# Where the P products of an attention-plus-FFN kernel run: two runs of 1024 columns a batch in place of four of 512

## The chip, the cores and the metric

The kernel runs on one core of one Trainium2 chip. The metric is the device time of one execution in microseconds (us). Before the change it is 701.11 us, the median of three runs that lie between 700.99 and 701.15 us.

## The reference

Eight batches of compressed-memory attention with 8 heads feed a feed-forward layer with SiLU:

```python
a = softmax(phi, over the sequence)             # phi: (8, 8, 576, 32)
k_m = einsum('bhsm,bhsd->bhmd', a, k)           # (8, 8, 32, 64)
v_m = einsum('bhsm,bhsd->bhmd', a, v)
attn = softmax(q @ k_m.T / sqrt(64))            # (8, 8, 576, 32)
x = attn @ v_m                                  # to (4608, 512)
h = x @ w_in                                    # (512, 2048)
out = (h * sigmoid(h)) @ w_out                  # (2048, 512)
```

All data are float32. The weights reach the chip as 64-bit words, which the kernel turns into float32 during the first batch.

## The kernel before, in words

**The algebra.** The kernel never forms x. For a batch b it forms P = v_m @ w_in, head by head: a matrix of 256 rows (8 heads of 32 memories) and 2048 columns, the hidden width. Then h = attn @ P. Each float32 factor of the two big products is split into a rounded part and a remainder ("hi" and "lo", type fp32r), and hi·hi + hi·lo + lo·hi is added up in PSUM.

**One iteration.** The work of a batch is 16 iterations, fc = 0 to 15, each for 128 hidden columns. On TensorE (PE) an iteration is, in program order:

1. `ffn1(b, fc)` (L637): 12 matmuls of 288 columns into the tile `h`, which is two PSUM banks; only columns 0 to 287 of each bank are used. There is one buffer of `h`, so the next `ffn1` waits until all readers of this one are done.
2. The events of the slots (b, fc) and (b, fc + 0.5): small steps that prepare this and the next batch.
3. `finish` (L676, `ffn2`): 12 matmuls of 512 columns for the iteration before, into four PSUM banks `acc`.

In batch 0 the order differs a little: half of `finish` comes before the events of part 0 and half before those of part 1. After each odd batch four more groups ("left", `accleft`) handle the 64 rows of two batches that the 512-row main part leaves over.

ScalarE (ACT) runs `silu`: L660 on the first 256 columns of both banks, then L662 on the last 32 (`gleft`). VectorE (DVE) makes hi (L652) and lo (L654) of the result, `gparts`. PE's instructions keep the program's order; from batch 1 on ACT's do too. DVE's order is drawn up by a scheduler at compile time, which may move an instruction ahead of one that was traced before it.

**The P products.** `p_mm(b, f, w)` (L602) makes w columns of P: 8 matmuls with 64-row, 32-column tiles of the array (4 head pairs by 2), run by PE as 16 instructions, into the two banks of the tile `bg`. `p_split` then has ACT copy them to hi (L616) and DVE subtract to get lo (L618), into `pparts`, which holds two blocks of 512 columns. A block j (512 columns) is used by `ffn1` of fc = 4j to 4j + 3.

**The slots.** From batch 1 on, block j = 1, 2, 3 is made at slot 4j − 3, that is at 1, 5 and 9, and block 0 of the next batch n = b + 1 at slot 14. For the next batch there are also, from batch 1 on, in slot 5 `e_mm` (L322, L330: k_m and v_m), in slot 9 `e_tr` (L352: their transposes), in slot 10 `s_all` (L367: the scores), in slot 12 `s_max` and `s_sub`, then `s_exp` (13), `s_sum`, `s_norm`, and in slot 14 `s_back` (L442, L443) and `s_low` (L448). In slots 5 and 9 the P product is registered first, so on PE it stands ahead of `e_mm` and of `e_tr`.

**Beside h.** `e_mm`, `e_tr` and part of `s_all` write into the unused columns of the same `h` tile that `ffn1` of that iteration has just filled:

```python
    def beside_h(w):
        return [live["h"][:, i, HALF : HALF + w] for i in range(2)]
```

Tiles are guarded by whole PSUM banks. In the built program the first matmul of `e_mm`, of `e_tr` and of the part of `s_all` beside h carries a wait for the L662 of the same iteration (ACT's last read of those banks).

**Stores.** `store` (L683) has ACT copy an `acc` bank to a tile `o`, one of three buffers that the raw weights used in batch 0, and the SP queue sends it out.

**The start.** In the first 30 us, products with an identity tile (`keep_warm`, L79) stand on PE wherever it waits for the first batch's attention; the longest such wait holds 13 of them (line 815).

Of the kernel before, what the change touches and what calls it, by code (L numbers as in the profile page):

```python
# [10 lines left out]
F32 = mybir.dt.float32  # L11
F32R = mybir.dt.float32r
# [7 lines left out]
P = 128  # L20
# [4 lines left out]
DMODEL, DFF = 512, 2048  # L25
NFC = DFF // P
CW = 256
JW = 512
NJ = DFF // JW
# [3 lines left out]
NI = MAIN // P  # L33
# [8 lines left out]
RAWB = 3  # L42
# [6 lines left out]
def attn_ffn_kernel(  # L49
# [9 lines left out]
    nc = tc.nc  # L59
    const = ctx.enter_context(tc.tile_pool(name="const", bufs=1))  # L60
    sb = ctx.enter_context(tc.tile_pool(name="sb", bufs=2))
    ps = ctx.enter_context(tc.tile_pool(name="ps", bufs=1, space=bass.MemoryType.PSUM))
# [4 lines left out]
    dummy = ident.bitcast(mybir.dt.bfloat16)  # L67
# [4 lines left out]
    gparts = const.tile([P, 2, 2, MAIN], F32R, name="gparts")  # L72
    gleft = const.tile([P, NFC, 2 * LEFT], F32, name="gleft")
    aparts = const.tile([P, 2, 2, 2 * S], F32R, name="aparts")
    pparts = const.tile([P, 2, 2, 2 * JW], F32R, name="pparts")

    def keep_warm(t, n):
        for _ in range(n):
            nc.tensor.matmul(  # L79
                t, dummy[:, :P], dummy.unsqueeze(1).broadcast_to([P, 2, 2 * P]),  # L80
                start=True, stop=True, skip_group_check=True,
            )

    loads = []

# [28 lines left out]
    def bgtile():  # L114
        return ps.tile([P, 2, 512], F32, tag="bg", name="bg", bufs=1)
# [96 lines left out]
    def load_phi(b):  # L212
        t = sb.tile([P, PHW], F32, tag="att", name=f"phi{b}")
        at[b]["e"] = t[:, : FULLC * HM].rearrange("p (g c f) -> p g c f", g=2, c=FULLC)
        at[b]["er"] = t[:, FULLC * HM :]
        at[b]["et"] = t
        w = FULLC * P
        for f in ((0, w), (2 * w, PHW), (w, 2 * w)) if b == 0 else ((0, PHW),):
            load(t[:, f[0] : f[1]], phi[b, :, f[0] : f[1]], queue=nc.scalar if f[0] == w else None)
# [367 lines left out]

    pj = {}  # L590

    def p_mm(b, f, w, low=True):
        j = f // JW
        if f % JW == 0:
            pj[b, j] = [pparts[:, k, j % 2].rearrange("p (g f) -> p g f", g=2) for k in range(2)]
        hi, lo = pj[b, j]
        c = slice(f % JW, f % JW + w)
        bg = bgtile()
        kvT = at[b]["kvT"]
        for r in range(NR):  # L600
            for p in range(2):
                nc.tensor.matmul(  # L602
                    bg[M * r : M * (r + 1), p, :w].rearrange("p (k f) -> p k f", f=P),
                    kvT[D * p : D * (p + 1), 1, r],
                    win[D * p : D * (p + 1), f // P : (f + w) // P, r],
                    start=True, stop=True, skip_group_check=True,
                )
        if low:
            p_split(b, f, w, bg)
        return bg  # L610

    def p_split(b, f, w, bg, steps=(0, 1)):
        hi, lo = pj[b, f // JW]
        c = slice(f % JW, f % JW + w)
        if 0 in steps:
            nc.scalar.activation(hi[:, :, c], bg[:, :, :w], AF.Copy)  # L616
        if 1 in steps:
            nc.vector.tensor_tensor(lo[:, :, c], bg[:, :, :w], hi[:, :, c], op=ALU.subtract)  # L618
# [47 lines left out]
            last_silu.append(i)  # L666
        return g32

    acc = {}

    def ffn2(gs, cs, fc, key):
        ghi, glo = gs
# [5 lines left out]
            )  # L678

    def store(key, rows, last=False):  # L680
        o = sb.tile([P, DMODEL], F32, tag="raw", name="o", bufs=RAWB)
        a = acc.pop(key)
        nc.scalar.activation(o, a, AF.Copy)  # L683
        at_ = 0
        for k, (r, n) in enumerate(rows):
            (nc.scalar if last and k else nc.sync).dma_start(out[r : r + n], o[at_ : at_ + n])
            at_ += n
# [17 lines left out]
    def ev(b, slot, fn, *a):  # L705
        events.setdefault((b, slot), []).append((fn, a))

    for b in range(B):
        n = b + 1
        if b == 0:  # L710
            for j in range(2, DFF // CW):
                ev(b, 2 * j - 1.5, p_mm, b, j * CW, CW)
        else:
            for j in range(1, NJ):
                ev(b, 4 * j - 3, p_mm, b, j * JW, JW)
        if n == B:
            continue
        at_slot = (4, 5, 6, 7.5, 9, 9.5, 11.5, 12.5, 13, 13.5, 13.5, 14) if b == 0 else (1, 2, 3, 5, 9, 10, 10, 11, 12, 13, 13, 14)
        mx, sub, ex, em, tr, s0, s1, sx, se, ss, sn, sk = at_slot
        ev(b, mx, phi_max, n)  # L720
        if n == 1:
            ev(b, sub, phi_allmax, n, (0, 1), (0,))
            ev(b, sub + 0.5, phi_allmax, n, (0, 1), (1,))
        else:
            for i in range(3):
                ev(b, sub, phi_fold, n, i)
        ev(b, sub + 0.5, phi_sub, n)
        ev(b, ex, phi_exp, n)
        ev(b, em, e_mm, n)
        if n + 1 < B:  # L730
            ev(b, 14 if b == 0 else em + 1, load_kv, n + 1)
        ev(b, tr, e_tr, n)
        ev(b, em, load_q, n, 1)
        if n == 1:
            ev(b, s0, s_mm, n, 0)
            ev(b, s1, s_mm, n, 1)
        else:
            ev(b, s0, s_all, n)
        if n + 1 < B:
            ev(b, s1, load_q, n + 1, 0)  # L740
        ev(b, sx, s_max, n, ALL)
        ev(b, sx, s_sub, n, ALL)
        ev(b, se, s_exp, n, ALL)
        ev(b, ss, s_sum, n, ALL)
        ev(b, sn, s_norm, n, ALL)
        ev(b, sk, s_back, n, ALL)
        ev(b, sk, s_low, n, ALL)
        if n + 1 < B:
            ev(b, sk, load_phi, n + 1)
        ev(b, 14, p_mm, n, 0, JW)  # L750
    slots = [1.5, 1.5] + [2 * j - 1 if k == "i" else min(2 * j - 0.5, 12.5) for k, i in later for j in [i - 1 if k == "i" else i]]
    to_do = list(slots)
    for slot in slots:
# [14 lines left out]
    with in_order(DVE, ACT) as last:  # L768
        load_phi(0)
        nc.scalar.activation(tiny[:, :1], ident[:, :1], AF.Exp)  # L770
        load_kv(0)
        for c in LOADS.split():
            if c[0] == "Q":
                load_q(0, int(c[1]), True)
            elif c[0] == "L":
                load_next(True)
            else:
                w_load((c[0], 0), int(c[1]), True)
        keep_warm(idle, 10)
        phi_max(0, (0,))  # L780
        phi_allmax(0, (0,))
        phi_max(0, (1,))
        keep_warm(idle, 3)
        phi_sub(0, (0,))
        phi_allmax(0, (1,))
        phi_sub(0, (1,))
        for p in range(2):
            phi_exp(0, (p,))
        keep_warm(idle, 2)
        e_mm(0)  # L790
        w_conv(I0, 0, "pc")
        keep_warm(idle, 3)
        f_tr()
        f_vt()
        w_conv(I0, 0, "s")
        keep_warm(idle, 2)
        f_scores(0)
        f_copy(0)
        w_conv(I0, 0, "a")
        spare = ps.tile([P, 512], F32, tag="acc", name="spare", bufs=NI)  # L800
        keep_warm(spare, 2)
        f_turn(0)
        f_scores(1)
        f_max(0)
        f_copy(1)
        f_sub(0)
        keep_warm(spare, 3)
        f_turn(1)
        f_exp(0)
        w_conv(I0, 1, "pc")  # L810
        f_max(1)
        f_sub(1)
        f_exp(1)
        nc.scalar.activation(tiny[:, :1], ident[:, :1], AF.Silu)
        keep_warm(spare, 13)
        f_sum(0)
        f_norm(0)
        w_conv(I0, 1, "sa")
        f_back(0)
        f_sum(1)  # L820
        w_conv(O0, 0, "p")
        f_high(0)
        w_conv(O0, 0, "c")
        keep_warm(spare, 3)
        bg = p_mm(0, 0, CW, False)
        keep_warm(spare, 5)
        p_split(0, 0, CW, bg, (0,))
        w_conv(I1, None, "p")
        f_norm(1)
        f_back(1)  # L830
        f_low(0)
        p_split(0, 0, CW, bg, (1,))
        f_high(2)
        f_high(1)
        w_conv(O0, 0, "sh")
        f_low(1)
        f_low(2)
        w_conv(O0, 0, "a")
        h = ffn1(0, 0, low_last=True)
        g32 = silu(0, 0, h)  # L840
        w_conv(I1, None, "cs")
        gs = split(g32, steps=(0,))
        w_conv(O0, 0, "l")
        split(g32, steps=(1,), gs=gs)
        g32 = silu(0, 1, ffn1(0, 1, bgtile()))
        w_conv(I1, None, "a")
        w_conv(O0, 1, "pc")
        main_step(0, 0, gs, (0, 1))
        g1 = split(g32, steps=(0,))
        w_conv(O0, 1, "s")  # L850
        p_mm(0, CW, CW)
        w_conv(O0, 1, "h")
        main_step(0, 0, gs, (2, 3))
        split(g32, steps=(1,), gs=g1)
        w_conv(O0, 1, "al")
        prev = ("main", 0, 1, g1)
# [25 lines left out]
    for b in range(B):  # L882
# [3 lines left out]
        for fc in range(NFC):  # L886
# [5 lines left out]
            h = ffn1(b, fc)  # L892
            gs = split(silu(b, fc, h))
            for part in range(2):
# [3 lines left out]
                n = len(traced)  # L898
# [72 lines left out]
```

## Time and profile before

| what | value |
|---|---|
| median of three runs | 701.11 us |
| span of the profiled execution | 700.3 us (the rest of its time, some 0.8 us by the median, lies around the span) |
| mean granted TensorE clock | 0.998 |
| PE busy | 689.4 us (98%) |
| DVE busy | 365.4 us (52%) |
| ACT busy | 259.0 us (37%) |
| DMA, mean | 86 GB/s |
| L676 main / L637 / left L676, share of the chain that ended last | 45% / 25% / 6% |
| L602 (P) busy | 35.8 us |

A row of the timeline gives the start and duration in us, engine, line, operation, out<-in with shapes, and the count of merged instructions; brackets name idle time of that engine just before, and what ended it. Matmuls are pipelined and their ends are modelled, so the time that a group takes from PE is read from its start to the next group's start, not from its duration. PEld is the weight load, which overlaps PE.

### The profile page before, as it was taken

How to read it: one execution, taken by the hardware profiler on the slowest of the kernel's cores; microseconds unless marked ns; L12 is line 12 of the kernel's file. 1: busy time of each engine (PE TensorE's matmuls, PEld its weight loads, DVE VectorE, ACT ScalarE, POOL GpSimd, SP SyncE). 2: the span in 40 equal slices, each digit the busy share in tenths (PEclk: the TensorE clock that was granted, in tenths of full speed). 3: DMA queues.
4: the chain of work that ended last, by engine and by line, in shares of the span. 5: the costliest groups of instructions: out<-in, count | busy, mean ns of one | idle time of the engine just before them, and what ended most of it. 6: DMA issues, size and time to landing. Idle time of an engine off the chain costs nothing.

```text
span 700.3 us, 11773 instructions
## 1 busy us (share of the span) xinstructions
PE 689.4 (98%) x4924; PEld 562.4 (80%) x4924; DVE 365.4 (52%) x665; ACT 259.0 (37%) x456; POOL 0.7 (0%) x6
## 2 busy tenths in 40 slices
PE   7999999999999999999999999999999999999997
PEld 3578777888888888888888888888888888888886
DVE  4898797435654256534636346542564525623322
ACT  3879584422424224421423314342241413431211
POOL 0000000000000000000000000000000000000000
PEclk9999999999999999999999999999999999999999
DMA  9995752212201221132110311112121000010002
GB/s 334 317 338 187 254 212 95 78 61 68 92 19 46 92 68 44 52 137 69 35 61 16 137 56 47 61 54 83 68 80 31 1 1 1 1 61 1 1 0 76
DMA packets 25445, 60.15 MB, mean 86 GB/s; under 512 B 2096, under 2 KB 10416, under 8 KB 25392
## 3 DMA queue, kind: packets, MB, share of 16 engines
q1 hardware_dynamic: 24448, 56.63, 22.8%
q10 hardware_dynamic: 944, 2.77, 1.1%
q8 instruction: 39, 0.64, 0.4%
q14 instruction: 14, 0.11, 0.1%
HBM read 49.95 MB, written 9.44 MB: 85 GB/s over the span
## 4 chain that ended last, share of the span: by engine, by line
PE 84%; DVE 2%; issue 0%; ACT 0%; ACTq 0%
PE acc L676 45%; PE h L637 25%; PE accleft L676 6%; PE bg L602 4%; PE h L322 2%; PE bg L367 1%; DVE wo_lo L176 0%; DVE raw L172 0%; PE h L330 0%; PE h L352 0%; DVE aparts L448 0%; DVE aT L442 0%; DVE gparts L654 0%; DVE sc L415 0%; DVE smx L411 0%
## 5 line engine op out<-in xcount | busy, mean ns | idle before, releaser
L676 PE MATMUL acc<-wo_hi,gparts 128*128 128x512 f32 x1024 | 341.8, 395 | 0.1
L676 PEld LDWEIGHTS acc<-wo_hi,gparts 128*128 128x128 f32 x1024 | 192.0, 188 | 52.7 <-issue 6.6
L637 PEld LDWEIGHTS h<-aparts,pparts 128*128 128x128 f32 x1524 | 214.0, 188 | 14.4 <-issue 2.1
L637 PE MATMUL h<-aparts,pparts 128*128 128x288 f32 x1524 | 223.3, 295 | 0.7 <-ACT aparts L581 0.4
L660 ACT ACTIVATE g<-h 128x512 f32<-128x512 f32 x127 | 76.0, 599 | 345.9 <-PE h L637 180.3
L676 PE MATMUL acc<-wo_lo,gparts 128*128 128x512 f32 x512 | 200.8, 392 | 0.7 <-DVE wo_lo L176 0.6
L652 DVE CAST gparts<-g 128x512 fp32r<-128x512 f32 x128 | 54.4, 425 | 260.0 <-ACT g L660 260.0
L676 PEld LDWEIGHTS acc<-wo_lo,gparts 128*128 128x128 f32 x512 | 96.1, 188 | 18.4 <-DVE wo_lo L176 1.9
L654 DVE TENSOR_TENSOR gparts<-g,gparts 128x512 fp32r<-128x512 f32 x128 | 88.2, 689 | 10.3
L618 DVE TENSOR_TENSOR pparts<-bg,pparts 128x1024 fp32r<-128x1024 f32 (+1 forms) x36 | 39.7, 1102 | 5.4 <-ACT pparts L616 5.0
L676 PE MATMUL accleft<-wo_hi,gparts 128*128 128x512 f32 x128 | 40.6, 389 | 0.0
L616 ACT ACTIVATE pparts<-bg 128x1024 fp32r<-128x1024 f32 (+1 forms) x36 | 33.6, 932 | 14.8 <-PE bg L602 14.8
L602 PE MATMUL bg<-win,kvT 64*32 64x512 f32 (+1 forms) x576 | 35.8, 554 | 0.0
L676 PEld LDWEIGHTS accleft<-wo_hi,gparts 128*128 128x128 f32 x128 | 24.0, 188 | 4.9
L662 ACT ACTIVATE gleft<-h 128x64 f32<-128x64 f32 x127 | 27.8, 219 | 0.0
L683 ACT ACTIVATE o<-acc 128x512 f32<-128x512 f32 x32 | 19.2, 600 | 21.8 <-PE acc L676 10.6
L676 PE MATMUL accleft<-wo_lo,gparts 128*128 128x512 f32 x64 | 24.9, 389 | 0.0
L660 ACT ACT_TABLE_LOAD x14 | 18.0, 1283 | 14.2 <-issue 13.6
L652 DVE CAST gparts<-gleft 128x512 fp32r<-128x512 f32 x16 | 6.8, 427 | 20.7 <-PE accleft L676 12.2
L168 ACT ACTIVATE raw<-raw 128x1024 int32<-128x1024 uint32 (+1 forms) x16 | 16.8, 1048 | 0.0
L322 PEld LDWEIGHTS h<-kv,phi 128*32 128x32 f32 x384 | 10.2, 110 | 5.0 <-ACT gleft L662 5.0
L676 PEld LDWEIGHTS accleft<-wo_lo,gparts 128*128 128x128 f32 x64 | 12.0, 188 | 2.4
(139 smaller groups left out, 365.0 us busy)
## 6 DMA issues: line engine op xcount, KB each, us to landing
kv<-in_kv SPq DMA_DIRECT2D x28, 516.0 KB, 5.9
q<-in_q SPq DMA_DIRECT2D x16, 576.0 KB, 5.7
out<-o SPq DMA_DIRECT2D x32, 256.0 KB, 2.1
raw<-in_w_in SPq DMA_DIRECT2D x14, 512.0 KB, 6.6
raw<-in_w_out SPq DMA_DIRECT2D x6, 1024.0 KB, 5.5
phi<-in_phi SPq DMA_DIRECT2D x7, 576.0 KB, 3.8
kv<-in_kv ACTq DMA_DIRECT2D x4, 516.0 KB, 6.8
kr<-in_kv SPq DMA_DIRECT2D x7, 258.0 KB, 6.4
```

Source lines behind the costliest of these rows:

```text
L168: nc.scalar.activation(r, low, AF.Copy, scale=2.0**-29)
L322: nc.tensor.matmul(pt[p][M * r : M * (r + 1), :KVW], e[:, p, c, M * r : M * (r + 1)], kvt[c][:, p, r], start=c == 0, stop=False, skip_grou ...
L602: nc.tensor.matmul(bg[M * r : M * (r + 1), p, :w].rearrange("p (k f) -> p k f", f=P), kvT[D * p : D * (p + 1), 1, r], win[D * p : D * (p + ...
L616: nc.scalar.activation(hi[:, :, c], bg[:, :, :w], AF.Copy)
L618: nc.vector.tensor_tensor(lo[:, :, c], bg[:, :, :w], hi[:, :, c], op=ALU.subtract)
L637: nc.tensor.matmul(h[:, hf, :HALF], wt[:, p, fs], a[:, p, hf * HALF : (hf + 1) * HALF], start=n[hf] == 0, stop=n[hf] == 5, skip_group_chec ...
L652: nc.vector.tensor_copy(ghi, g32)
L654: last_split.append(nc.vector.tensor_tensor(glo, g32, ghi, op=ALU.subtract))
L660: nc.scalar.activation(g32.rearrange("p (h f) -> p h f", h=2), h[:, :, :w], AF.Silu)
L662: i = nc.scalar.activation(gleft[:, fc, o : o + LEFT].rearrange("p (h f) -> p h f", h=2), h[:, :, w:HALF], AF.Silu)
L676: nc.tensor.matmul(acc[key], gt[:, cs], wt[:, fc], start=fc == 0 and n == 0, stop=fc == NFC - 1 and n == 2)
L683: nc.scalar.activation(o, a, AF.Copy)
```

## The change

1. From batch 1 on P is made in runs of two blocks. `p_run(b, j)` sends the 16 instructions of block j into `bg` and the 16 of block j + 1 into a newly allocated `h` tile, all 512 columns of each bank; then block j + 1 is split first (so that `h` comes free) and block j second. `p_run(b, 2)` stands in slot 6 of batch b; `p_run(n, 0)` for the next batch in slot 12 (slot 14 of batch 0). Nothing is made any more in slots 1, 5, 9 and (after batch 0) 14. Batch 0's own P products are unchanged.
2. Blocks 0 and 1 have a home of their own (`early`, two of the three raw-weight buffers); blocks 2 and 3 stay in `pparts`.
3. `store` uses four fixed quarters of the third raw-weight buffer in turn.
4. The 13 identity products of line 815 are replaced by 16 products of zeros or of 96 identity columns, of 128 to 512 columns each, and two identity products; GpSimd (POOL) zeroes a part of `gparts` for them at the start.

```diff
+    nc.gpsimd.memset(gparts[:, 0, 0].bitcast(F32), 0.0)
+    zeros = gparts[:, 0, 0]
...
+    def zero_mm(t, k, n, w):
+        a = dummy if k == "half" else zeros
+        m = 96 if k == "half" else P
+        b = dummy.unsqueeze(1).broadcast_to([P, 2, 2 * P]) if k == "half" else zeros[:, :w]
+        for _ in range(n):
+            nc.tensor.matmul(t[:m, :w], a[:, :m], b, start=True, stop=True, skip_group_check=True)
...
-    pj = {}
-
-    def p_mm(b, f, w, low=True):
+    pj, early = {}, []
+
+    def p_home(b, j):
+        if b and j < 2:
+            if not early:
+                early.extend(sb.tile([P, 2, 2 * JW], F32R, tag="raw", name=f"pe{k}", bufs=RAWB) for k in range(2))
+            home = [early[k][:, j] for k in range(2)]
+        else:
+            home = [pparts[:, k, j % 2] for k in range(2)]
+        pj[b, j] = [x.rearrange("p (g f) -> p g f", g=2) for x in home]
+
+    def p_run(b, j):
+        bg = p_mm(b, j * JW, JW, False)
+        h = p_mm(b, (j + 1) * JW, JW, False, ps.tile([P, 2, 512], F32, tag="h", name="hp", bufs=1))
+        p_split(b, (j + 1) * JW, JW, h)
+        p_split(b, j * JW, JW, bg)
+
+    def p_mm(b, f, w, low=True, bg=None):
...
     def store(key, rows, last=False):
-        o = sb.tile([P, DMODEL], F32, tag="raw", name="o", bufs=RAWB)
+        if not homes:
+            homes.append(sb.tile([P, NI, DMODEL], F32, tag="raw", name="o", bufs=RAWB))
+        o = homes[0][:, next(stored) % NI]
...
         else:
-            for j in range(1, NJ):
-                ev(b, 4 * j - 3, p_mm, b, j * JW, JW)
+            ev(b, 6, p_run, b, 2)
...
+        PR = 14 if b == 0 else 12
...
+        ev(b, PR, p_run, n, 0)
         ev(b, sx, s_max, n, ALL)
         ev(b, sx, s_sub, n, ALL)
...
-        ev(b, 14, p_mm, n, 0, JW)
...
-        keep_warm(spare, 13)
+        zero_mm(spare, "full", 3, 512)
+        zero_mm(spare, "full", 4, 256)
+        zero_mm(spare, "half", 3, 512)
+        zero_mm(spare, "full", 3, 288)
+        zero_mm(spare, "full", 3, 128)
+        keep_warm(spare, 2)
```

More of the change, by code (lines that the diff above doesn't have):

```diff
@@ L586, in attn_ffn_kernel @@
     ALL = (0, S)
-    pj = {}
-    def p_mm(b, f, w, low=True):
+    pj, early = {}, []
[13 more added lines that the diff above has]
+    def p_mm(b, f, w, low=True, bg=None):
         j = f // JW
         if f % JW == 0:
[L595 to L598, printed above, removed]
+            p_home(b, j)
+        if bg is None:
+            bg = bgtile()
         kvT = at[b]["kvT"]
@@ L667, in silu @@
         return g32
-    acc = {}
+    acc, homes, stored = {}, [], iter(range(1 << 30))
     def ffn2(gs, cs, fc, key):
```

## The prediction

> **What bounds the kernel now.** I read the page first, then the table of windows, then PE's timeline around the places that the change touches, and last the waits of PE's weight loads.
>
> ```profile
> PE 689.4 (98%) x4924; PEld 562.4 (80%) x4924; DVE 365.4 (52%) x665; ACT 259.0 (37%) x456; POOL 0.7 (0%) x6
> ```
>
> ```profile
> 180.00:260.00 80.00, 80.00 (x568) 66.91 (x568) 37.16 (x73) 22.18 (x44) 0.00 (x0) 1.00 0.20 69
> 260.00:340.00 80.00, 80.00 (x590) 66.74 (x589) 40.28 (x77) 28.91 (x51) 0.00 (x0) 1.00 0.19 66
> ```
>
> PE is busy for all 80.00 us of a window of 80, at a granted clock of 1.00, while DVE and ACT stand idle half the time and more. So whatever PE does, or waits for, is paid in full, and whatever shortens only DVE, ACT or a queue gives nothing. The question is then how many microseconds each placed P product takes from PE, and this is read from start to start. First a plain iteration, then one with a P product alone (slot 1), in PE's timeline:
>
> ```profile
> 275.74 1.75 PE L637 MATMUL h<-aparts,pparts 128*128 128x288 f32 x12
> 277.33 0.39 PE L676 MATMUL acc<-wo_hi,gparts 128*128 128x512 f32 x1
> ...
> 280.07 1.74 PE L637 MATMUL h<-aparts,pparts 128*128 128x288 f32 x12
> 281.74 1.09 PE L602 MATMUL bg<-win,kvT 64*32 64x512 f32 x16
> 282.76 0.50 PE L676 MATMUL acc<-wo_hi,gparts 128*128 128x512 f32 x1
> ...
> 285.61 1.75 PE L637 MATMUL h<-aparts,pparts 128*128 128x288 f32 x12
> ```
>
> The plain iteration takes 280.07 − 275.74 = 4.33 us. With P it is 5.54, so P costs 1.21: entry 0.08 (1.67 to P instead of 1.59), body 1.02, exit 0.11 (2.85 to the next L637 instead of 2.74). Next, the same for slot 5 (P, then `e_mm`) and slot 9 (P, then `e_tr`):
>
> ```profile
> 131.79 1.74 PE L637 MATMUL h<-aparts,pparts 128*128 128x288 f32 x12
> 133.46 1.09 PE L602 MATMUL bg<-win,kvT 64*32 64x512 f32 x16
> 134.48 1.97 PE L322 MATMUL h<-kv,phi 128*32 128x129 f32 x64
> ...
> 139.63 0.42 PE L637 MATMUL h<-aparts,pparts 128*128 128x288 f32 x2
> ```
>
> ```profile
> 152.61 1.74 PE L637 MATMUL h<-aparts,pparts 128*128 128x288 f32 x12
> 154.28 1.09 PE L602 MATMUL bg<-win,kvT 64*32 64x512 f32 x16
> 155.30 0.44 PE L352 MATMUL h<-ident,kvn 128*128 128x128 f32 x2
> ...
> 158.33 0.42 PE L637 MATMUL h<-aparts,pparts 128*128 128x288 f32 x2
> ```
>
> These iterations take 7.84 and 5.72 us, 3.51 and 1.39 over the plain one. The four P slots of a batch (1, 5, 9, 14) cost 1.21 + 3.51 + 1.39 + 1.21 = 7.32, `e_mm` and `e_tr` included.
>
> **The cover that the move takes away.** Three narrow windows on PE, ACT's timeline of the same iteration, and the waits of the weight loads:
>
> ```profile
> 154.06 0.29 PE L637 MATMUL h<-aparts,pparts 128*128 128x288 f32 x1
> 154.28 0.66 PE L602 MATMUL bg<-win,kvT 64*32 64x512 f32 x8
> 154.73 0.64 PE L602 MATMUL bg<-win,kvT 64*32 64x512 f32 x8
> ```
>
> ```profile
> 154.93 0.22 ACT L662 ACTIVATE gleft<-h 128x64 f32<-128x64 f32 x1
> 155.47 1.03 ACT L616 ACTIVATE pparts<-bg 128x1024 fp32r<-128x1024 f32 x1 [0.33 <-PE bg L602]
> ```
>
> ```profile
> PEld h L322 <- ACT gleft L662: 5.0, 6, 0.8
> PEld h L352 <- ACT gleft L662: 5.0, 6, 0.8
> ```
>
> `e_mm` and `e_tr` write into banks that L660 and L662 still read, and wait for L662: in all six batches their weight load follows 0.8 us of idle time that L662 ended. L662 ends at 155.15, that is 1.09 after the start of the last L637 matmul (154.06). The P product runs from 154.28 to 155.30 and covers all of this. So P in slots 5 and 9 takes time that PE could not have used for the step behind it. In the changed kernel no P stands there, and since PE keeps program order nothing else can slip in. How soon PE follows L662 is seen at batch 1's start, where PE did idle for it:
>
> ```profile
> 107.90 0.22 ACT L662 ACTIVATE gleft<-h 128x64 f32<-128x64 f32 x1
> ```
>
> ```profile
> 108.17 0.53 PE L637 MATMUL h<-aparts,pparts 128*128 128x288 f32 x2
> 108.97 1.60 PE L637 MATMUL h<-aparts,pparts 128*128 128x288 f32 x10 [0.26 <-DVE aparts L448]
> ```
>
> 108.12 to 108.17: 0.05. So `e_mm` alone starts 1.09 + 0.05 = 1.14 after the last L637 start; behind P it started 1.24 after it (0.22 + 1.02). Removing P saves 0.10 in slot 5, not 1.02, and the same in slot 9: 3.41 and 1.29 remain. The lower bound of these two is an unhindered start, 2.49 and 0.29 (P's 1.02 gone, in slot 9 the entry too); the upper one 0.1 more in each, if changing the tile shape takes its 0.08 to 0.12 again after the wait. I take the wait without that, since the built program has it and the array can be drained by then.
>
> The Trainium skill, "PSUM — Partial Sum Buffer", section "PSUM bank collisions raise a hardware error", says that the chip does not arbitrate two engines on one bank and quadrant, disjoint columns included, so a semaphore must keep them apart. By that rule this wait cannot be scheduled away, and the trace agrees (155.15 before 155.30).
>
> **What a run of two costs.** One pass of 8 instructions takes 154.73 − 154.28 = 0.45 us, and behind the last pass 0.57, so 0.12 drains. A run is 0.08 + 4 × 0.45 + 0.12 + 0.11 = 2.12, against 2 × 1.21 apart: 0.30 saved. Its second half needs `h` free, at 1.14 by the same count, and the first half ends at 0.22 + 0.91 = 1.13. I add 0.05 (0.01 if weights load ahead, 0.11 if an entry is paid again): 2.17.
>
> Behind it the next `ffn1` needs `h` back. The copy starts 0.17 after the stream ends (155.47 against 155.30), takes 1.03, and DVE's subtraction takes 1.22:
>
> ```profile
> 135.71 1.22 DVE L618 TENSOR_TENSOR pparts<-bg,pparts 128x1024 fp32r<-128x1024 f32 x1 [0.24 <-ACT pparts L616]
> ```
>
> With two hand-overs of 0.05 that is 2.52 after the stream's end, and PE has 2.85 of L676 to do: 0.33 to spare, so nothing is added from batch 1 on.
>
> **Batch 0.** The run in slot 14 adds two passes, 0.91. But there only six L676 stand between it and the next `ffn1`, from 102.14 to 103.64:
>
> ```profile
> 101.13 1.09 PE L602 MATMUL bg<-win,kvT 64*32 64x512 f32 x16
> 102.14 0.50 PE L676 MATMUL acc<-wo_hi,gparts 128*128 128x512 f32 x1
> ...
> 103.64 1.75 PE L637 MATMUL h<-aparts,pparts 128*128 128x288 f32 x12
> ```
>
> ```profile
> 104.29 0.68 DVE L654 TENSOR_TENSOR gparts<-g,gparts 128x512 fp32r<-128x512 f32 x1
> 104.89 1.43 DVE L442 STREAM_TRANSPOSE aT<-sc 128x576 f32<-128x576 f32 x2
> 106.25 1.18 DVE L618 TENSOR_TENSOR pparts<-bg,pparts 128x1024 fp32r<-128x1024 f32 x1
> 107.56 1.36 DVE L448 TENSOR_TENSOR aparts<-aT,aparts 128x1152 fp32r<-128x1152 f32 x1
> ```
>
> PE would reach `ffn1` at 104.55. The run ends at 101.13 + 1.92 = 103.05, the copy at 104.25. DVE's subtraction stands behind L654 (the code ties it there in batch 0), so it runs from 104.97 to 106.19 and PE goes on at 106.24: 1.7 us lost. If the scheduler leaves L442 ahead of it, as before, 3.0; if it goes ahead of L654, 1.0. The chain through L442 and L448 to batch 1's first `ffn1` moves by about as much as PE does, so I add nothing there.
>
> **The small edits.** Stores: four buffers should end ACT's waits for outgoing DMAs, but PE hardly noticed them:
>
> ```profile
> PEld acc L676 <- ACT o L683: 0.8, 1, 0.8
> ```
>
> With no P in slot 1 PE needs `acc` 1.2 us sooner, and without the DMA wait it is free sooner too. Nothing. The raw buffers that `early` takes are last read by batch 0's weight conversion, which stands ahead of L654 on DVE; I add nothing for them. The zero products stand in a wait that a DVE chain ends:
>
> ```profile
> 18.62 2.97 PE L79 MATMUL spare<-ident 128*128 128x512 bf16 x13
> 22.46 0.63 PE L563 MATMUL firsta<-ident,fsc 128*128 128x128 f32 x4 [0.87 <-DVE fsc L556]
> ```
>
> PE is idle for 0.87 us behind them. 18 products at 0.23 each, the rate of a full L676, would be 4.1 of the 3.84 there: at most +0.3, and many are narrower, so zero. POOL's one fill (its whole busy time is 0.7) is ready long before 18 us.
>
> **The sum**, against the profiled execution's span of 700.3:
>
> - Batches 1 to 6, each: 2 × 2.17 + 3.41 + 1.29 = 9.04 for 7.32, +1.72; six times: +10.3.
> - Batch 7 (slots 1, 5, 9 had P alone): 2.17 for 3.63: −1.5.
> - Batch 0: +0.9 and +1.7.
>
> Together +11.4: a span of 711.7. The median of 701.11 stands 0.8 above the span, so 712.5.
>
> **Rivals.**
>
> 1. *The waits do not bite* (faster). If `e_mm` and `e_tr` could start at once, and `h` came back in time in batch 0 too, a batch costs 2 × 2.12 + 2.49 + 0.29 = 7.02, −0.30; six of these, −1.5 of batch 7 and +0.9 of batch 0 give −2.4: 698.7. With batch 0's stall 700.4. It decides if PE starts L322 and L352 less than 0.3 us behind L637. For it speaks only that no iteration of before shows PE itself idle there; against it the twelve waits above. A rule for it is in the Trainium skill, "TensorEngine Tiling (Array Packing)", section "Key Properties": changing the tiling mode drains TensorE. By it fewer changes of mode are a gain, and the trace agrees on their price (0.08 to 0.12 each); it does not see the cover.
> 2. *`h` comes back late in every run* (slower still). The spare is 0.33. If DVE is in the middle of a long step when the copy ends, up to 1.36 − 0.33 = 1.0 is lost; with this in the six slot-12 runs, 718.5. `s_max` and `s_sub` are traced right behind that run, but before they ran far earlier, in slots 10 and 11:
>
> ```profile
> 163.54 1.35 DVE L411 TENSOR_REDUCE smx<-sc 128x36 f32<-128x1152 f32 x1
> 164.92 1.36 DVE L415 TENSOR_TENSOR sc<-sc,smx 128x1152 f32<-128x1152 f32 x1
> ```
>
> 3. *The run costs nothing more than its passes, and the exposure is half*: the scheduler finds ACT's reads of `h` sooner ended, 0.5 instead of 1.0 exposed: 12 × 0.5 less, 706.5. Nothing in the trace speaks for it: L660 starts as soon as L637 ends.
>
> **Chances and range.** The forecast holds 0.8 (own range 710 to 715.5, from the bounds 0.01 to 0.11 on 13 runs, 1.0 to 3.0 in batch 0 and the 0.3 at the start); rival 1 has 0.07, rival 2 0.08, rival 3 0.05. A measurement here tells 0.2% (1.4 us) from no change. Rival 1 is faster in most of its cases, the same in the rest: faster 0.05, same 0.03, slower 0.92. The range goes from 707, toward rival 3, to 717, toward rival 2.
>
> **What would show it.** Right: PE idle about 0.9 to 1.0 us before L322 and L352, ended by L662, in each of batches 1 to 6; iterations 5 and 9 of 7.7 and 5.6 us; runs of 32 instructions of about 1.9 us, with no gap behind L676; PE idle some 1.7 us in batch 0's last iteration, ended by DVE's L618 line. PE busy then falls below 98%. Wrong: L322 or L352 close behind L637 (then rival 1), or a gap before L637 behind each run (rival 2).

## The result, and the profile after

The changed kernel takes 718.4 us (four runs, 717.12 to 718.95) against 701.09 us of the kernel before on the same chip: the ratio is 1.0242, with a 95% interval of 1.0227 to 1.0256. It is slower, as forecast, but by 17.3 us where 11.4 were forecast, and outside the range of 707 to 717. The profiled execution has a span of 715.3 us, a time of 717.12 and a mean granted clock of 1.000.

The page's busy times after:

```profile
PE 690.3 (96%) x4929; PEld 563.8 (79%) x4929; DVE 365.1 (51%) x665; ACT 259.1 (36%) x456; POOL 1.2 (0%) x7
```

PE has 0.9 us more to do in a span 15.0 longer; the rest, 14.1, is idle time of PE. Three rows of PE's waits, with the sum, the count and the longest in us, name 13.5 us of it:

```profile
PE h L331 <- ACT gleft L685: 5.1, 6, 0.9
PE h L361 <- ACT gleft L685: 5.1, 6, 0.9
PE h L660 <- DVE pe L641: 3.3, 1, 3.3
```

Line numbers moved: L625 is the P product (L602 before), L660 `ffn1` (L637), L699 `ffn2` (L676), L331 and L339 `e_mm`, L361 `e_tr`, L683 and L685 the two parts of silu, L639 and L641 the split of P. The tile `pe` is the new home of blocks 0 and 1. This is PE's timeline of slots 5 and 6 of batch 2, and then of slot 9:

```profile
226.15 1.75 PE L660 MATMUL h<-aparts,pe 128*128 128x288 f32 x12
228.75 1.97 PE L331 MATMUL h<-kv,phi 128*32 128x129 f32 x64 [0.85 <-ACT gleft L685]
...
233.91 1.75 PE L660 MATMUL h<-aparts,pe 128*128 128x288 f32 x12
235.59 1.09 PE L625 MATMUL bg<-win,kvT 64*32 64x512 f32 x16
236.53 1.09 PE L625 MATMUL hp<-win,kvT 64*32 64x512 f32 x16
...
240.39 1.75 PE L660 MATMUL h<-aparts,pe 128*128 128x288 f32 x12
...
249.07 1.74 PE L660 MATMUL h<-aparts,pparts 128*128 128x288 f32 x12
251.66 0.44 PE L361 MATMUL h<-ident,kvn 128*128 128x128 f32 x2 [0.85 <-ACT gleft L685]
...
254.69 0.55 PE L660 MATMUL h<-aparts,pparts 128*128 128x288 f32 x3
```

Slot 5 takes 233.91 − 226.15 = 7.76 (7.84 before), slot 9 5.62 (5.72 before), although 16 instructions of P are gone from each: in their place PE idles 0.85 us until L685 has read `h`. The iteration with the run in slot 6 takes 6.48, or 2.15 over the 4.33 of a plain one, and no gap stands before the L660 behind it.

The table sets the forecast's terms beside the trace, with three places that the forecast had at nothing. It goes from start to start of `ffn1` in the two traces; the share of the home of blocks 0 and 1 is the difference to the version of the experiments in which these blocks lie at another address. The first row of the table is the start of fc = 14 of batch 0, before and after:

```profile
98.06 1.75 PE L637 MATMUL h<-aparts,pparts 128*128 128x288 f32 x12
```

```profile
99.20 1.75 PE L660 MATMUL h<-aparts,pparts 128*128 128x288 f32 x12
```

| place | forecast, us | measured, us |
|---|---|---|
| start, up to fc = 14 of batch 0 | 0 | +1.1 (98.06 to 99.20) |
| run in batch 0: fc = 14 to fc = 15 | +2.6 | +4.3 (5.58 to 9.90) |
| end of batch 0, first iterations of batch 1 | 0 | −0.9 |
| moved steps, batches 1 to 6 | +10.3 | +10.0 (six times 1.66) |
| batch 7 | −1.5 | −1.5 |
| home of blocks 0 and 1, batches 1 to 7 | 0 | +2.0 (seven times 0.28) |
| sum: the span | +11.4 | +15.0 (700.3 to 715.3) |

### The profile page after: what moved, and what is told of

Read it like the earlier page. It is cut to its first block, busy times and chain, and to the rows that moved or that the text cites. A ratio compares the mean times of both kernels' runs of the same rounds, so it can differ in the third digit from the quotient of the medians.

```text
span 715.3 us, 11784 instructions
## 1 busy us (share of the span) xinstructions
PE 690.3 (96%) x4929; PEld 563.8 (79%) x4929; DVE 365.1 (51%) x665; ACT 259.1 (36%) x456; POOL 1.2 (0%) x7
## 4 chain that ended last, share of the span: by engine, by line
PE 78%; issue 5%; DVE 2%; ACT 1%; ACTq 0%
PE acc L699 42%; PE h L660 22%; PE accleft L699 6%; PE bg L625 2%; PE hp L625 2%; PE h L331 2%; ACT g L683 1%; PE bg L376 1%; PE h L361 0%; DVE wo_lo L185 0%; DVE raw L181 0%; PE h L339 0%; DVE pe L641 0%; ACT gleft L685 0%; DVE gparts L677 0%
## 5 line engine op out<-in xcount | busy, mean ns | idle before, releaser
L699 PE MATMUL acc<-wo_hi,gparts 128*128 128x512 f32 x1024 | 342.6, 395 | 0.1
L699 PEld LDWEIGHTS acc<-wo_hi,gparts 128*128 128x128 f32 x1024 | 192.1, 188 | 51.5 <-issue 7.5
L699 PE MATMUL acc<-wo_lo,gparts 128*128 128x512 f32 x512 | 201.0, 393 | 1.0 <-DVE wo_lo L185 1.0
L683 ACT ACTIVATE g<-h 128x512 f32<-128x512 f32 x127 | 76.0, 598 | 342.3 <-issue 175.8
L660 PEld LDWEIGHTS h<-aparts,pparts 128*128 128x128 f32 x852 | 119.3, 188 | 12.8 <-DVE pe L641 3.7
L660 PE MATMUL h<-aparts,pparts 128*128 128x288 f32 x852 | 125.4, 296 | 3.7 <-DVE pe L641 3.3
L699 PEld LDWEIGHTS acc<-wo_lo,gparts 128*128 128x128 f32 x512 | 96.1, 188 | 19.1 <-DVE wo_lo L185 2.4
L660 PEld LDWEIGHTS h<-aparts,pe 128*128 128x128 f32 x672 | 95.0, 188 | 4.9
L660 PE MATMUL h<-aparts,pe 128*128 128x288 f32 x672 | 98.1, 295 | 0.0
L699 PE MATMUL accleft<-wo_hi,gparts 128*128 128x512 f32 x128 | 40.7, 390 | 0.0
L699 PEld LDWEIGHTS accleft<-wo_hi,gparts 128*128 128x128 f32 x128 | 24.0, 188 | 4.9
L685 ACT ACTIVATE gleft<-h 128x64 f32<-128x64 f32 x127 | 27.8, 219 | 0.0
L699 PE MATMUL accleft<-wo_lo,gparts 128*128 128x512 f32 x64 | 24.9, 390 | 0.0
L625 PE MATMUL bg<-win,kvT 64*32 64x512 f32 (+1 forms) x352 | 20.5, 523 | 0.0
L331 PE MATMUL h<-kv,phi 128*32 128x129 f32 x384 | 11.8, 275 | 5.1 <-ACT gleft L685 5.1
L641 DVE TENSOR_TENSOR pparts<-bg,pparts 128x512 fp32r<-128x512 f32 (+1 forms) x15 | 14.0, 935 | 2.9 <-ACT pparts L639 2.8
```

The costliest lines, as they stand in the source:

```text
L331: nc.tensor.matmul(pt[p][M * r : M * (r + 1), :KVW], e[:, p, c, M * r : M * (r + 1)], kvt[c][:, p, r], start=c == 0, stop=False, skip_grou ...
L625: nc.tensor.matmul(bg[M * r : M * (r + 1), p, :w].rearrange("p (k f) -> p k f", f=P), kvT[D * p : D * (p + 1), 1, r], win[D * p : D * (p + ...
L660: nc.tensor.matmul(h[:, hf, :HALF], wt[:, p, fs], a[:, p, hf * HALF : (hf + 1) * HALF], start=n[hf] == 0, stop=n[hf] == 5, skip_group_chec ...
L683: nc.scalar.activation(g32.rearrange("p (h f) -> p h f", h=2), h[:, :, :w], AF.Silu)
L685: i = nc.scalar.activation(gleft[:, fc, o : o + LEFT].rearrange("p (h f) -> p h f", h=2), h[:, :, w:HALF], AF.Silu)
L699: nc.tensor.matmul(acc[key], gt[:, cs], wt[:, fc], start=fc == 0 and n == 0, stop=fc == NFC - 1 and n == 2)
```

## The experiments

Each is an edit of the changed kernel unless it says that it is one of the kernel before. A ratio is always to the kernel before, run beside it on the same chip (its medians: 702.02 us for the first four, 701.49 for the next four, 702.17 for the last four).

**Cover for `e_mm` and `e_tr`.** Blocks 2 and 3 are made singly again, in the slots of `e_mm` and `e_tr` and ahead of them.

```diff
-            ev(b, 6, p_run, b, 2)
+            ev(b, 5, p_mm, b, 2 * JW, JW)
+            ev(b, 9, p_mm, b, 3 * JW, JW)
```

> The changed kernel, but blocks 2 and 3 are made one at a time again, ahead of e_mm (slot 5) and ahead of e_tr (slot 9), and not as a run in slot 6. The run of blocks 0 and 1 stays in slot 12. Theory (the cover): PE's waits for L685 before e_mm and e_tr, 10.2 us in all, are gone. A batch of 1 to 6 costs 3.51 + 1.39 + 2.16 for these steps instead of 9.03, 1.97 less, six times 11.8; batch 7 costs 2 x 1.21 instead of 2.15, 0.3 more: the span falls by 11.5 to 703.8. Rival (the loss lies in the runs as such, in their use of h): only one of two runs is gone, and the span falls by about half of the loss, to 708 to 710.

Measured: 707.13 us, ratio 1.0074 (1.0057 to 1.0091), span 705.4. PE's timeline of slot 5 of batch 2:

```profile
225.62 1.75 PE L660 MATMUL h<-aparts,pe 128*128 128x288 f32 x12
227.31 1.09 PE L625 MATMUL bg<-win,kvT 64*32 64x512 f32 x16
228.32 1.97 PE L331 MATMUL h<-kv,phi 128*32 128x129 f32 x64
...
233.45 1.75 PE L660 MATMUL h<-aparts,pe 128*128 128x288 f32 x12
```

The iteration with P and `e_mm` takes 7.83, only 0.07 more than that with `e_mm` alone in the changed kernel, and the idle time is gone. Two blocks of P ride in slots 5 and 9 for 0.07 + 0.10, where the run in slot 6 costs 2.15. Each of batches 1 to 6 falls by 1.94, batch 2 from 79.90 to 77.96, its time in the kernel before (what the slower home costs there, the joined run in slot 12 saves). This is the forecast mechanism, shown by undoing it: it carries two thirds of the loss. The span stayed 1.6 above the expected 703.8; 1.5 of that is a clock drop behind batch 0's wait (below), which the profiled execution of the changed kernel does not have.

**Batch 0's run.** The run that batch 0 makes for batch 1 is taken apart: block 0 in slot 14 as before, block 1 in slot 1 of batch 1.

```diff
-        ev(b, PR, p_run, n, 0)
+        if b:
+            ev(b, PR, p_run, n, 0)
...
+        if b == 0:
+            ev(b, 14, p_mm, n, 0, JW)
+            ev(n, 1, p_mm, n, JW, JW)
```

> The changed kernel, but the first run, that of batch 0, is taken apart: block 0 alone in slot 14 of batch 0, into bg only, and block 1 alone in slot 1 of batch 1. Theory: PE's one wait of 3.3 us for DVE's L641 before the last ffn1 of batch 0 is gone, since h is no longer lent there; against it stand 0.3 us for a second entry and exit. Part of it comes back as waits of batch 1's first ffn1 for L457, 0.3 us as before. The span falls by 2.4 to 3.0, to 712.3 to 712.9. Rival (DVE is late there anyway, and batch 1's first iteration waits instead): it falls by less than 1.

Measured: 715.28 us, ratio 1.0191 (1.0176 to 1.0207), span 713.1. In the changed kernel PE, ACT and DVE stand like this at that place:

```profile
103.14 1.06 PE L625 MATMUL hp<-win,kvT 64*32 64x512 f32 x16
...
105.40 0.40 PE L699 MATMUL acc<-wo_hi,gparts 128*128 128x512 f32 x1
109.10 1.86 PE L660 MATMUL h<-aparts,pparts 128*128 128x288 f32 x12 [3.30 <-DVE pe L641]
```

```profile
103.45 1.02 ACT L639 ACTIVATE pe<-bg 128x1024 fp32r<-128x1024 f32 x1 [0.43 <-PE bg L625]
104.38 1.02 ACT L639 ACTIVATE pe<-hp 128x1024 fp32r<-128x1024 f32 x1
```

```profile
106.03 0.77 DVE L451 STREAM_TRANSPOSE aT<-sc 128x576 f32<-128x576 f32 x1
106.73 1.18 DVE L641 TENSOR_TENSOR pe<-bg,pe 128x1024 fp32r<-128x1024 f32 x1
107.84 1.21 DVE L641 TENSOR_TENSOR pe<-hp,pe 128x1024 fp32r<-128x1024 f32 x1
```

The run splits `hp` first, since PE waits for that. In batch 0, where order is not fixed, the scheduler put `bg` first on both engines, and one L451 ahead of both. On DVE the L451 and the subtraction of `bg` take 0.70 and 1.11 us ahead of that of `hp`, from start to start. PE's L660 waits behind all of it, 3.3 us. With the run taken apart the step from fc = 14 to fc = 15 is that of before:

```profile
99.28 1.74 PE L660 MATMUL h<-aparts,pparts 128*128 128x288 f32 x12
102.34 1.09 PE L625 MATMUL bg<-win,kvT 64*32 64x512 f32 x16
104.86 1.75 PE L660 MATMUL h<-aparts,pparts 128*128 128x288 f32 x12
```

That is 5.58 in place of 9.90. Some 2 us of the 4.3 came back: batch 1 pays 1.2 for the single block in slot 1, and its start is again as slow as before (0.7 of it had hidden behind the wait). That the order of the splits makes the wait is read from the trace; forcing the other order in batch 0 wasn't tried.

**No fill, no zero products.** The identity products of before, and GpSimd's fill dropped.

```diff
-    nc.gpsimd.memset(gparts[:, 0, 0].bitcast(F32), 0.0)
-    zeros = gparts[:, 0, 0]
...
-        zero_mm(spare, "full", 3, 512)
...
-        keep_warm(spare, 2)
+        keep_warm(spare, 13)
```

> The changed kernel with the 13 identity products at the start as before, and without POOL's fill of gparts. Theory (a queue at the start): the fill stood on POOL between the two steps that make the identity tile, which came 0.42 us later; ACT's first instruction reads it, and the DMAs of k and v are issued behind that on ACT's queue. Then POOL's identity step ends at 1.30 us again, e_mm of batch 0 takes 3.1 us instead of 3.6, batch 0 runs 0.6 to 1.1 us earlier, and the span falls to 714.2 to 714.7. Rival (the differences of the start are chance between runs): the start stays where it is, or moves without that order. The time around the span, 1.8 us in the changed kernel and 0.8 before, goes back to 0.8 if the zero products or the fill cause it, and stays at 1.8 otherwise.

Measured: 717.73 us, ratio 1.0225 (1.021 to 1.0241), span 716.4. The start did get shorter, fc = 14 of batch 0 at 97.69 in place of 99.20, and yet the span is longer. The table of windows (per 4 us: busy times of PE, PEld, DVE, ACT, POOL; then the granted clock, DMA share and GB/s) of this version shows what took it:

```profile
108.00:112.00 4.00, 4.00 (x16) 3.71 (x16) 1.99 (x3) 1.88 (x3) 0.00 (x0) 0.50 0.48 147
112.00:116.00 4.00, 4.00 (x20) 3.45 (x19) 0.69 (x1) 0.00 (x0) 0.00 (x0) 0.82 0.02 4
```

The granted clock falls to 0.50 right in and behind batch 0's wait. The iteration behind the wait takes 7.11 us, from 107.57 to 114.68, with its L660 (here L658) drawn out to 3.25:

```profile
107.57 3.25 PE L658 MATMUL h<-aparts,pparts 128*128 128x288 f32 x12 [3.28 <-DVE pe L639]
114.68 1.76 PE L658 MATMUL h<-aparts,pe 128*128 128x288 f32 x12
```

In the changed kernel's profiled execution it takes 4.44, and the window stays at 1.00:

```profile
108.00:112.00 4.00, 2.90 (x18) 2.70 (x19) 2.77 (x3) 1.88 (x3) 0.00 (x0) 1.00 0.28 56
```

So it is in the version with cover, where that iteration takes 5.98:

```profile
108.00:112.00 4.00, 3.03 (x12) 3.03 (x13) 2.77 (x3) 1.16 (x1) 0.00 (x0) 0.62 0.32 82
```

Seven traces have the wait, of 3.28 to 3.30 us by the modelled ends. In the five of edited versions the clock drops behind it and the iteration takes 5.76 to 7.25; in the two of the changed kernel itself (one is the repeat below) it stays at 1.00. Where the wait is missing it stays at 1.00 there in every version, before included. The Trainium skill, "TensorE: Matmul & The Clock Gate", Part 1, says that TensorE's clock is gated to half after an idle window of about 3.4 us. The traces agree in kind, and put 3.3 us of idle time at the edge, where one execution drops and another doesn't.

**Blocks 0 and 1 at a multiple of 64 bytes.** In the changed kernel an iteration with weights from `pe` takes 4.37, one from `pparts` 4.33. In the built program the two tiles of `pe` start at 196640 and 180256, both 32 bytes past a multiple of 128, and `pparts` at 136064, a multiple of 128. A tile allocated ahead of `pe` is made 8 floats longer, which moves it by 32 bytes.

```diff
-        t = sb.tile([P, NR, KVW], F32, tag="kr", name=f"kr{b}", bufs=1)
+        t = sb.tile([P, NR * KVW + 8], F32, tag="kr", name=f"kr{b}", bufs=1)[:, : NR * KVW].rearrange("p (r f) -> p r f", r=NR)
```

> The changed kernel, with one buffer made 32 bytes longer, so that the raw-weight buffers (and early in them) start at a multiple of 64 bytes instead of 32 past one. Theory 1 (address): iterations whose weights come from early took 4.37 us in the changed kernel against 4.33 with pparts; the 32 bytes cause it, and the iterations 0 to 7 come down to 4.33: the span falls by 7 x 8 x 0.04 = 2.2 us, from 715.3 to about 713. Rival (the place high in the buffer memory, or that hi and lo lie in two tiles): they stay at 4.37 and the span at 715.3.

Measured: 719.21 us, ratio 1.0251 (1.0233 to 1.0268), span 719.5. A miss: the iteration came down to 4.36 only, and this execution lost 1.3 us more at the start and dropped its clock behind batch 0's wait (0.50 in 112 to 116 us).

**The changed kernel again**, with no edit, to see whether its own spread is the clock.

> The changed kernel itself once more, for comparison with its neighbours on the same chip. Theory (clock): PE's idle stretch of 3.3 us in batch 0's last iteration lies at the edge of what makes the clock drop to half. Spans fall into two groups, about 715.3 with a mean clock of 1.000 and 716.5 to 718 with 0.994 to 0.998, and in the second the granted clock behind that stretch is 0.5 for some microseconds. Rival: the spread has another place, and the clock there stays 1.0.

Measured: 718.52 us, ratio 1.0241 (1.0225 to 1.0256). One run has a span of 715.4 at a mean clock of 1.000, three have 716.6 to 716.9 at 0.996 to 0.998. The trace is that of the first, so the drop itself was not seen window by window in the unedited kernel. A mean of 0.998 alone does not show it either: the profiled execution of before has that too, with 1.00 in all windows from 96 to 120 us. But the longer spans, by 1.2 to 1.5 us, fit the drop in the version with cover (5.98 − 4.44 = 1.5).

**A multiple of 128 bytes.** As above, but 28 floats longer, which moves `pe` by 96 bytes, to 196736 and 180352.

> The changed kernel, with one buffer 112 bytes longer, so that early starts at a multiple of 128 bytes, as pparts does. With 64 the iterations took 4.36. Theory (128 bytes): iterations 0 to 7 take 4.33, and the span falls by 2.2. Rival (the place as such, not its remainder): they stay at 4.36 to 4.37.

Measured: 716.5 us, ratio 1.0218 (1.0201 to 1.0235), span 714.5 with a clock drop of 1.3 us in it. Two `ffn1` in succession at the start of batch 2 in PE's timeline, first of the changed kernel, then of this one (between the two stands the 64-byte version, 208.46 to 212.82):

```profile
204.32 1.75 PE L660 MATMUL h<-aparts,pe 128*128 128x288 f32 x12
208.69 1.75 PE L660 MATMUL h<-aparts,pe 128*128 128x288 f32 x12
```

```profile
205.18 1.75 PE L660 MATMUL h<-aparts,pe 128*128 128x288 f32 x12
209.51 1.75 PE L660 MATMUL h<-aparts,pe 128*128 128x288 f32 x12
```

4.37 with the home as it was, 4.36 at 64 bytes, 4.33 at 128. Batches 1 to 7 fall by 0.28 each, batch 2 from 79.90 to 79.62.

**The homes swapped.** Blocks 2 and 3 take `pe`, blocks 0 and 1 `pparts`. (The last iteration of batch 0 then reads block 1 of batch 1 in place of its own block 3, so these 128 columns of the hidden width come out as others; the steps are the same.)

```diff
-        if b and j < 2:
+        if b and j > 1:
...
-            home = [early[k][:, j] for k in range(2)]
+            home = [early[k][:, j % 2] for k in range(2)]
```

> The changed kernel with the homes exchanged: blocks 0 and 1 in pparts, blocks 2 and 3 in early. Theory (place): the slow iterations go with the place, so that iterations 0 to 7 take 4.33 us and 8 to 15 take 4.37; the span stays within 0.5 of the changed kernel's. Rival (something else in the first half of a batch is slow): iterations 0 to 7 stay at 4.37.

Measured: 719.17 us, ratio 1.0254 (1.0239 to 1.027), span 716.7. The slow iterations move with the place, from fc 0 to 7 to fc 8 to 15:

```profile
210.13 1.75 PE L660 MATMUL h<-aparts,pparts 128*128 128x288 f32 x12
214.46 1.75 PE L660 MATMUL h<-aparts,pparts 128*128 128x288 f32 x12
...
245.97 1.75 PE L660 MATMUL h<-aparts,pe 128*128 128x288 f32 x12
250.33 1.75 PE L660 MATMUL h<-aparts,pe 128*128 128x288 f32 x12
```

4.33 with `pparts`, 4.36 with `pe`. So it is the place, not the block, the slot or what runs beside it.

**Three edits in one**: cover, batch 0's run apart, no fill and no zero products.

> The changed kernel with three of its parts taken back at once: blocks 2 and 3 alone ahead of e_mm and e_tr, batch 0's run taken apart (block 0 in slot 14, block 1 in slot 1 of batch 1), and the identity products of the start as before without POOL's fill. What is left: the runs of blocks 0 and 1 in slot 12 of batches 1 to 6, the homes in early, the store buffers. Theory: against the kernel before, six runs at 2.16 for two P products apart at 2.42 save 1.6 us, and 56 iterations that read their weights from early cost 0.04 more each, 2.2 us: a span of 700.9, no change that can be told. Rival (runs in h's banks cost by themselves): a span over 703.

Measured: 701.51 us, ratio 1.0001 (0.9992 to 1.001), span 699.5, clock 1.0. The three take away the whole difference to before; the joined run that is left in slot 12 and the slower home of blocks 0 and 1 cancel out.

**The fourth added.** The same with the 28 floats.

> Against the changed kernel: the singles of blocks 2 and 3 ahead of e_mm and e_tr, batch 0's run taken apart, no fill and no zero products (all three as in the version that took 701.51 us, span 699.5), and the raw copy of k and v 28 floats longer, so that blocks 0 and 1 of P lie at a multiple of 128 bytes. If the address is worth 0.04 us in each of the 56 iterations that read these two blocks, the iterations of fc 0 to 7 take 4.327 in place of 4.367 and the span falls by 56 x 0.04 = 2.2 us, to 697.3, some 699.2 in all: 0.3% under the kernel before. If the 0.04 comes from something else that merely went along with the padding, the span stays at 699.5 and the time at the 701.5 of before.

Measured: 700.22 us, ratio 0.9973 (0.9962 to 0.9984), span 698.2. This is the fastest version, 0.3% ahead of the kernel before. PE is busy for 687.9 us, 99% of the span. PE's timeline of two iterations with `pe`:

```profile
202.50 1.75 PE L658 MATMUL h<-aparts,pe 128*128 128x288 f32 x12
206.83 1.75 PE L658 MATMUL h<-aparts,pe 128*128 128x288 f32 x12
```

4.33 again. From fc = 14 of batch 0 to the end it takes some 1.8 us less than the version with three edits (seven batches at 0.22 to 0.31; the expectation's 56 iterations at 0.04, 2.2 us, are too many, since slots with other work lose less), and some 1.7 less than before: six runs at 2.16 in place of two singles at 1.21 each, 0.26 a run, are 1.6. That is the saving of joined passes that the change could have had.

**The kernel before with the padding alone**, as a control.

> The kernel before, with nothing changed but 28 floats of padding behind the raw copy of k and v. If the padding acts only through the home of blocks 0 and 1, which this kernel does not have, the time is that of before within 0.2 us and an iteration takes 4.327 as before. If it moved some other operand to a better place, the time falls with it, by up to the 2.2 us seen on the changed kernel.

Measured: 702.19 us, ratio 0.9999 (0.999 to 1.0007). Nothing: the padding acts only through the home of blocks 0 and 1.

**The kernel before with the four store buffers alone.**

```diff
-        o = sb.tile([P, DMODEL], F32, tag="raw", name="o", bufs=RAWB)
+        if not homes:
+            homes.append(sb.tile([P, NI, DMODEL], F32, tag="raw", name="o", bufs=RAWB))
+        o = homes[0][:, next(stored) % NI]
```

> The kernel before, with nothing changed but the four fixed store buffers of the change. The theory that the stores cost nothing either way: the 9.8 us in which ACT waits for a buffer's DMA vanish from its waits, PE's do not move, the time is that of before within 0.3 us. Its rival, that ACT's wait for a buffer delays the next silu somewhere: the time falls by some part of 9.8 us, at least 0.5.

Measured: 701.76 us, ratio 0.9995 (0.9986 to 1.0003). This row of before's waits has no counterpart in this version's:

```profile
ACT o L683 <- DMA out<-o: 9.8, 8, 2.4
```

Nearly ten microseconds of waiting left ACT, and the time is the same within the measurement.

**The kernel before with the fill and the zero products alone.**

```diff
+    nc.gpsimd.memset(gparts[:, 0, 0].bitcast(F32), 0.0)
+    zeros = gparts[:, 0, 0]
...
-        keep_warm(spare, 13)
+        zero_mm(spare, "full", 3, 512)
...
+        keep_warm(spare, 2)
```

> The kernel before, with nothing changed but the start: GpSimd fills the part of gparts, and the 16 zero products and two identity products replace the 13. If the fill stands between the two steps of the identity and ACT's first instruction waits for that, the kv transfers leave 0.4 to 0.5 us later and the first e_mm runs that much later; fc = 14 of batch 0 starts 0.5 to 1.5 us after the 98.06 of before and the time is 701.5 + 0.5 to 1.5. If the zero products are what counts (their sum is shorter or longer than the wait that they fill, or the clock goes with them), the first e_mm starts as in before and the difference appears only behind them. If the start is free, within 0.2 us.

Measured: 703.4 us, ratio 1.002 (1.0011 to 1.0029), span 701.9. The timeline of all engines at the start, of this version and then of before, with one row of PE from some 10 us later:

```profile
0.87 0.53 POOL L76 MEMSET gparts<- 128x512 f32 x1
...
1.43 0.29 POOL masks.py:199 TENSOR_SCALAR_AFFINE_SELECT ident<-ident 128x128 f32<-128x128 f32 x1
1.76 0.82 ACTq L96 DMA_DIRECT2D kv<-in_kv  x2
...
13.35 0.42 PE L339 MATMUL first<-kr,phi 64*32 64x129 f32 x11
```

```profile
1.01 0.29 POOL masks.py:199 TENSOR_SCALAR_AFFINE_SELECT ident<-ident 128x128 f32<-128x128 f32 x1
...
1.34 1.39 ACTq L87 DMA_DIRECT2D kv<-in_kv  x3
...
12.27 0.45 PE L330 MATMUL first<-kr,phi 64*32 64x129 f32 x16
```

The scheduler put the fill between the two steps that make the identity. In both kernels ACT's queue issues the kv transfers 0.04 us after the identity's last step ends (1.72 and 1.30): 0.42 later here, and the last part of batch 0's `e_mm` is 1.08 later. That is ahead of the zero products, which stand at 19.64 us. They themselves add about 0.1 (3.94 us to the next L572 in place of 3.84), PE then waits for the converted weights of w_out 0.4 longer (1.0 in all against 0.6), and fc = 14 comes at 99.60 against 98.06. So 1.1 of the 1.5 us arise behind the fill and ahead of the products. Why the delay grows from 0.42 at the issue to 1.08 is not shown, nor what lengthens the wait for w_out, and no version has the fill without the products. Over all versions, fc = 14 starts at 97.18 to 98.06 in the six without a fill and at 99.05 to 100.54 in the eight with it.

## Why the prediction was right about the direction and wrong about the size

**The lost cover: right.** PE idles 0.85 us before L331 and L361, ended by L685, in each of batches 1 to 6. The four steps of a batch were priced at 9.04 against 7.32, +1.72; where the home costs nothing (the 128-byte version) they measure +1.66. Slots 5 and 9 came out at 7.76 and 5.62 (forecast 7.74 and 5.62), the runs at 2.15 and 2.16 (2.17). Batch 7 was −1.5 and is −1.5.

**Rivals 1 and 3: false.** The waits bite, in full. **Rival 2: false.** No run from batch 1 on delays the `ffn1` behind it. The time landed near the 718.5 of rival 2 for other reasons.

**Batch 0's stall: mis-sized.** The forecast said 1.7, with 3.0 as the upper end, and it is 3.3. The step that failed is the order on DVE: I let the subtraction of `hp` follow L654 at once, and as the upper end only L442 stood ahead of it. That the scheduler might split `bg` first, on ACT and on DVE, was in neither end; that subtraction alone is 1.11 us. The code traces `hp` first, and I took that for the order.

**Batch 1's start: mis-sized the other way.** "Moves by about as much as PE does" was counted as nothing; the longer wait hid 0.7 us of delays that before had stood there. Most of the other 0.1 to 0.2 is in slot 3 of batch 1, which takes 4.45 in the profile of before and 4.36 in that of before with the padding alone: it differs between executions, and is not the change's doing.

**"The small edits … zero": wrong in one.** The fill was judged by POOL's busy time and by the time at which its result is needed, 18 us. The question was what stands behind it on its own queue at 0.9 us: the identity, and with it the kv transfers on ACT's queue. It came to 1.1 us in the profiled execution, if the start is the fill's doing as far as the order in the traces tells. The stores were right at nothing, and so were the zero products, nearly (0.1).

**The home of blocks 0 and 1: left out.** Its cost was sought in who last reads the raw buffers. The address of the place was not considered; it costs 2.0 us over the kernel.

**The clock: left out.** The windows of before that I read show 1.00, and I priced an idle PE only at its own length. Behind a wait of 3.3 us the granted clock may halve: 1.3 to 2.8 us more in the traces that show it, and most likely the 1.3 us by which the median of 718.4 stands above the profiled 717.12.

**Outside the span: 0.8 for 1.8.** The 0.8 us was the median of before less the span of one profiled execution. In every execution with both numbers on record, of before as of the other versions, the time lies 1.73 to 1.86 us above the span. So this is not the change's doing: most likely the profiled execution of before itself took some 702.1 us, 1.0 over the median; its own time is not on record.

**All of it.** The span missed by 3.6: batch 0's run +1.7, batch 1's start −0.9, the start +1.1, the home +2.0, the moved steps −0.3. From the forecast of 712.5 these 3.6, the 1.0 around the span and the 1.3 of clock make 718.4. The start and the home, 3.1 together, had been put at nothing. Two sums of the forecast are off by less: a run adds up to 2.11, not 2.12, and the bounds named for its own range give 711.3 to 714.9, not 710 to 715.5.

## What to carry to other kernels

Work that stands in another's wait costs almost nothing there (0.07 to 0.10 us here for 16 instructions of 1.02 us) and its full length anywhere else: before joining small steps into one, see what each of them covers. An added instruction is to be priced on its own queue, by what is behind it there, however small and however early it is ready; and where a scheduler draws up the order, both orders belong in the bounds. A new buffer has an address, and an idle stretch has a clock behind it.

## What the runs showed of the hardware

- The place of TensorE's stationary operand matters beyond what the program must keep to. 24 matmuls of an iteration take 4.367 us with the weights (fp32r, blocks of 128 columns) at 32 bytes past a multiple of 128, 4.360 at 64 past it, and 4.327 at a multiple of 128 (medians; the addresses are read from the built program). The Trainium skill, "SBUF — State Buffer", section "Operand start alignment", asks only for a multiple of the element's size and says that this is about legality and timed nothing. The runs put a price beside it. Why the difference also shows in the L699 of these iterations, which read other operands (2.777 against 2.743 us), stays open.
- An idle stretch of 3.3 us on PE is at the edge of the clock gate: behind it the granted clock of a window of 4 us fell to between 0.50 and 0.76 in five traces, and stayed at 1.00 in two.
